# A decode kernel's weight loads: 16 rows of one load per layer moved to three transfer engines, and W2's last 64 rows loaded over 16

## The chip, the cores and the metric

The kernel runs on one core of one Trainium2 chip. The metric is device time in microseconds (us) of one execution; lower is better. The five engines of a core are called PE (matrix products; PEld is its weight load), DVE (vector), ACT (scalar, which also issues loads), POOL and SP (which only issues loads here). Loads from the chip's main memory are carried out by 16 transfer engines that all issuers share.

## The reference

One token goes twice through an attention block with a cache of 8192 positions and an MLP. All is float32.

```python
def _A_ref(x, k_cache, v_cache, wq, wo):            # x [1, 1, 640]; caches [1, 32, 8192, 128]
    q = (x @ wq).reshape(B, Sq, H, Dh).transpose(0, 2, 1, 3)     # 32 heads of 128
    scores = jnp.einsum("bhqd,bhkd->bhqk", q, k_cache) * (Dh ** -0.5)
    p = softmax(scores)
    o = jnp.einsum("bhqk,bhkd->bhqd", p, v_cache)
    return o.transpose(0, 2, 1, 3).reshape(B, Sq, H * Dh) @ wo   # wo [4096, 640]

def _B_ref(x, w1, w2):                              # w1 [640, 1728], w2 [1728, 640]
    return jnp.maximum(x @ w1, 0) @ w2

x = A_x
for layer in range(2):                              # both layers: the same caches and weights
    x = x + _A_ref(layernorm(x), k_cache, v_cache, wq, wo)
    x = x + _B_ref(layernorm(x), w1, w2)
```

K and V of one layer have 268 MB, so the caches alone, read once per layer, are most of the 573.76 MB that the kernel moves.

## The kernel before

**The stream of K and V.** SP issues nearly nothing but loads of K and V into `ring`, one large buffer of 128 partitions (`pump`, L264). A load has 128 rows of 4 to 64 KB. The order of these loads is a list written ahead (`todo`); SP issues the next one as soon as its place in the ring is free, which PE sets by reading the pieces that lay there (`release`). Layer 0 goes through the heads 0 to 31, layer 1 through 31 to 0, so that the pieces of the last heads are kept from one layer to the next.

**A head.** For each head PE forms the scores (`scores`, L540), DVE and ACT the softmax (`exponentials`: L551, L556, L563, L565, L569, L571), PE the sum over V (`values`, L595; `late_values`, L613, for the last one), and DVE and PE its output column (L628 to L646).

**The weights of attention.** Heads stand in eight groups of four. `pair` is one buffer of 128 partitions with two halves, each for the weights of one group: `wqo` holds Wq and Wo of the eight groups side by side, so laid out that one load of two neighbouring groups brings Wo of one group and Wq of the next. Such a load (`load_pair`, L323, issued by ACT) has 128 rows of 2 x 10240 = 20480 bytes. When a group's first head is through, `run_out` multiplies the outputs of the group before with Wo (`projected`, L510) and then issues the next load into `pair`; two heads later `queries_by_halves` (L467, L476, L481) reads Wq of the group after. In layer 0 the first group of a load counts 0, 1, 2 and so on, in layer 1 it counts down.

**W1 and W2.** They are loaded once, in layer 0, by ACT, as the function `due` tells by the head's place: W1 (L838), most of the W2 rows that stay (L840, 128 rows), and W2's last 64 rows (L843). W2's other rows come in each layer through the ring as the last of SP's loads, and the last blocks of the MLP read them (`times_rows`, L498). The last 64 rows are stored in DRAM as two blocks of 8 x 5 rows, of which 8 x 4 are read; so each of the two loads has 32 rows of 2560 bytes, in eight runs of four.

**What sets the order.** Each engine works its instructions off in the order in which the program wrote them. A load gives a signal when all its bytes have landed. There are eight such signals (`DMAHW0` to `DMAHW7` in the listings below); all loads of SP and ACT use them in turn, and a load waits for the one that had its signal eight loads before.

Of the kernel before, what the change touches and what calls it, by code (L numbers as in the profile page):

```python
# [15 lines left out]
P = 128  # L16
D = 640
# [7 lines left out]
NG = H // HG  # L25
# [65 lines left out]
]  # L91
KEPT = 4024
W2_PLACES = 800
WIDE = 64
MIX_BEHIND = 3
MIX_AT = [10, 14, 18, 22]
# [19 lines left out]
def size(unit):  # L116
    return sum(wide(kind_of(unit, t), piece) for t, piece in enumerate(unit[1]))
# [4 lines left out]
F_TILES = 3  # L122
# [5 lines left out]
W2_ALL = [("w2", i) for i in range(len(W2_RUNS))]  # L128
RING = KEPT + W2_PLACES


@with_exitstack
def decode_kernel(ctx: ExitStack, tc: tile.TileContext, x, kv, wqo, w1, w2, w2_rest, w2_last, out):
    nc = tc.nc
    consts = ctx.enter_context(tc.tile_pool(name="consts", bufs=1))
    work = ctx.enter_context(tc.tile_pool(name="work", bufs=1))
# [60 lines left out]
    for row in ROWS:  # L197
        n = 8 * sum(size(UNITS[h][i]) for h, i in row)
        block = kv[o : o + P * n].rearrange("(p m) -> p m", p=P)
        o += P * n  # L200
        a = 0
# [4 lines left out]
    for u in W2_ALL:  # L206
        n = 8 * P * size(UNITS[u[0]][u[1]])
# [91 lines left out]
    pair = consts.tile([P, 2, NB * HG * DH], F32, name="pair")  # L299

    def chain(g, i):

        return (g + i) % 2

    def as_wq(half):
        return pair[:, half].rearrange("p (c n) -> p c n", c=NB)

    def as_wo(half):
        return pair[:, half].rearrange("p (j n) -> p j n", j=HG)

    def load_wq(g, queue):
        wq_t[g] = as_wq(1)
        queue.dma_start(pair[:, 1], wqo[chain(g, 0)][:, g])

    def load_pair(g_o, g_q):

        if g_q is None:
            n = D if g_o == 0 else 0
            nc.scalar.dma_start(pair[:, 0, n:], wqo[chain(g_o, 1)][:, g_o, n:])
            wo_t[g_o] = as_wo(0)  # L320
            return
        first = min(g_o, g_q)
        nc.scalar.dma_start(  # L323
            pair.rearrange("p a n -> p (a n)"),
            wqo[chain(g_o, 1)][:, first : first + 2].rearrange("p a n -> p (a n)"),
        )
        wo_t[g_o] = as_wo(g_o - first)
        wq_t[g_q] = as_wq(g_q - first)

# [25 lines left out]
    w2_t = consts.tile([P, F_REST, D], F32, name="w2_t")  # L355
# [300 lines left out]
    def sums_of_rows(pt, rows, last, some=range(4)):  # L656
        for r in some:
            nc.tensor.matmul(
                pt[:, :WIDE],
                rows[:, r],  # L660
                ind[:, r : r + 1].to_broadcast([P, WIDE]),
                start=(r == 0),
# [77 lines left out]
    def attention_and_mlp(L, xr, s):  # L740
# [3 lines left out]
        groups = [run[0] // HG for run in runs]  # L744
# [14 lines left out]
        if L:  # L759
            load_wq(groups[1], nc.scalar)  # L760
        else:
            load_pair(groups[0], groups[1])

        chores, slow = [], []

# [12 lines left out]
        def run_out(k):  # L778

            projected(times_halves, acc, runs[k], o_cols[k], k == 0, k == NG - 2)  # L780
            yield "dve"
            load_pair(groups[k + 1], groups[k + 2] if k + 2 < NG else None)
            if k < NG - 2:
                return
            rows = work.tile([P, RUN], F32, name="p")[:64, : 2 * DR]
            nc.vector.tensor_copy(rows, acc[:64, : 2 * DR])
            pt = ps_m.tile([P, 512], F32, name="px")
            for g in range(4):
                nc.tensor.matmul(
                    pt[32 * g : 32 * g + 32, :DR],  # L790
                    sel[:64, g // 2 : g // 2 + 1].to_broadcast([64, 32]),
                    rows[:, g % 2 * DR : (g % 2 + 1) * DR],
                    start=True,
                    stop=True,
                )
            yield "dve"
            nc.vector.scalar_tensor_tensor(xr, pt[:, :DR], 1.0, xr, op0=ALU.mult, op1=ALU.add)
# [26 lines left out]
        def due(h):  # L824

            where = heads.index(h)
            k, j = divmod(where, HG)
            if j == 0:
                o_cols[k] = work.tile([P, HG], F32, name="o_cols", bufs=2)
                sums[k] = work.tile([P, 4 * HG], F32, name="sums", bufs=2)  # L830
            if where and j == 0:
                chores.append([run_out(k - 1), "pe"])
            if j == 2 and k + 1 < NG:
                slow.append([queries_of(k + 1), "pe"])
            if where == H - 2:
                chores.append([first_of_last(), "pe"])
            if L == 0 and where == 4:
                nc.scalar.dma_start(w1_t, w1)  # L838
            if L == 0 and where == 7:
                nc.scalar.dma_start(w2_t[:, 0], w2_rest)  # L840
            if L == 0 and where in (12, 13):
                a = 32 * (where - 12)
                nc.scalar.dma_start(w2_t[a : a + 32, 1], w2_last[where - 12, :, :4])  # L843
            if where == 7:
                of, nth = divmod(last, HG)
                if L:
                    make_identity(nc, ident)
                    n = D // 8
                    assert is_free(RING - n, n)
                    live["last"] = RING - n, n  # L850
                raw = ring[:, 8 * RING - D :] if L else mix[:, :D]
                nc.scalar.dma_start(raw, wqo[chain(of, 1)][:, of, nth * D : (nth + 1) * D])
                wo_last.append(raw if L else as_wo(0)[:, nth])
            if where == 8:
                slow.append([mixing(wo_last[-1] if L else mix[:, :D]), "dve"])
            if where in MIX_AT:
                slow.append([mixing_quarter(MIX_AT.index(where)), "pe"])
# [21 lines left out]
        for where, h in enumerate(heads[:-1]):  # L879
# [24 lines left out]
            k, j = divmod(where, HG)  # L904
# [14 lines left out]
            if near_end:  # L919
                rows = copied_rows(hd)  # L920
# [43 lines left out]
        rows = copied_rows(hd)  # L964
        at_once(rest)
        pt = ps_m.tile([P, 512], F32, name="pm")
        for a, (piece, at) in enumerate(pieces[2:]):
# [6 lines left out]
        nc.tensor.matmul(  # L974
            pt[:, :WIDE], o_late, one_of_each.to_broadcast([P, WIDE]), start=False, stop=True
        )
# [18 lines left out]
        for j in range(F_TILES):  # L995
            pj = bank_tile() if j else ps_m.tile([P, 512], F32, name="pt")
            nc.tensor.matmul(
                pj[:, :WIDE].rearrange("p (a g) -> p a g", g=4),
                hr[:, j * P : (j + 1) * P],
                sel[:, None, :4].to_broadcast([P, WIDE // 4, 4]),  # L1000
                start=True,
# [42 lines left out]
        for a, b in enumerate(blocks):  # L1044
# [13 lines left out]
            rows = 2 * half if b == nb + 1 else P  # L1058
            if b < nb:
                i = next(i for i, run in enumerate(W2_RUNS) if b in run)  # L1060
                where = L, ("w2", i), b - W2_RUNS[i][0]
                tile_of, at = at_of[where]
# [45 lines left out]
def _laid_out(A_x, A_k_cache, A_v_cache, A_wq, A_wo, B_w1, B_w2):  # L1108
    k = np.asarray(A_k_cache)[0].reshape(H, 4, 4, RUN, DH).transpose(0, 4, 1, 2, 3)
    v = np.asarray(A_v_cache)[0].reshape(H, 4, 4, NBL, 4, 32, DH)  # L1110
    v = v.transpose(0, 1, 5, 4, 2, 3, 6).reshape(H, P, 4, 4, NBL, DH)
    kv = np.empty(H * P * SK * 2, k.dtype)
    o = 0
    for row in ROWS:
        n = 8 * sum(size(UNITS[h][i]) for h, i in row)
        block = kv[o : o + P * n].reshape(P, n)
        o += P * n
        a = 0
        for h, i in row:
            unit = UNITS[h][i]  # L1120
            for t, piece in enumerate(unit[1]):
                if kind_of(unit, t) == "k":
                    r, c, m = piece
                    part = k[h, :, :, r, c : c + m]
                else:
                    b, r, m = piece
                    part = v[h, :, :, r : r + m, b]
                part = part.reshape(P, -1)
                block[:, a : a + part.shape[1]] = part
                a += part.shape[1]  # L1130
    rows = np.zeros((P, FB, D), np.asarray(B_w2).dtype)
    for b, f in enumerate(_hidden_rows()):
        rows[f >= 0, b] = np.asarray(B_w2)[f[f >= 0]][:, _COLS]
    w2 = np.concatenate([rows[:, run[0] : run[-1] + 1].reshape(-1) for run in W2_RUNS])
    wq = np.asarray(A_wq).reshape(NB, P, NG, HG * DH).transpose(2, 1, 0, 3).reshape(NG, P, -1)
    wo = np.asarray(A_wo)[:, _COLS].reshape(NG, HG, DH, D).transpose(0, 2, 1, 3).reshape(NG, P, -1)
    wqo = np.empty((2, P, NG, wq.shape[2]), wq.dtype)
    for g in range(NG):
        wqo[g % 2, :, g] = wq[g]
        wqo[1 - g % 2, :, g] = wo[g]  # L1140
    w2_last = np.zeros((2, 8, 5, D), rows.dtype)
    w2_last[:, :, :4] = rows[:64, 4 * F_TILES + 1].reshape(2, 8, 4, D)
    return {
        "x": np.repeat(np.asarray(A_x).reshape(D)[_COLS].reshape(4, DR), 32, axis=0),
        "kv": kv,
        "wqo": wqo,
        "w1": np.asarray(B_w1).reshape(NB, P, DFF).transpose(1, 0, 2),
        "w2": w2,
        "w2_rest": rows[:, 4 * F_TILES],
        "w2_last": w2_last,  # L1150
    }


# [22 lines left out]
```

## Time and profile before

| | |
|---|---|
| median of 3 runs | 1345.72 us (1345.54 to 1348.48) |
| the profiled execution | 1345.14 us, of which the span from the first to the last instruction is 1343.4 |
| busy, share of the span | PE 63%, PEld 20%, DVE 18%, ACT 4%, POOL 0% |
| moved | 573.76 MB, mean 427 GB/s |
| chain that ended last | DMA 62%, PE 28%, DVE 6% |

A page's DMA share is the mean busy share of the 16 transfer engines: 1.00 means that all work, 0.50 that eight do. It can read a little over 1 in a short stretch. `q1` is the queue of SP's loads, `q10` that of ACT's, `q8` and `q14` bring the program's own instructions. Each of the 16 engines has its own share of each queue, and one that has work from two queues takes from them in turn. In the chain, a line is a step that released the next one. The PE column of the clock says what share of its full speed PE was granted.

### The profile page before, as it was taken

How to read it: one execution, taken by the hardware profiler on the slowest of the kernel's cores; microseconds unless marked ns; L12 is line 12 of the kernel's file. 1: busy time of each engine (PE TensorE's matmuls, PEld its weight loads, DVE VectorE, ACT ScalarE, POOL GpSimd, SP SyncE). 2: the span in 40 equal slices, each digit the busy share in tenths (PEclk: the TensorE clock that was granted, in tenths of full speed). 3: DMA queues.
4: the chain of work that ended last, by engine and by line, in shares of the span. 5: the costliest groups of instructions: out<-in, count | busy, mean ns of one | idle time of the engine just before them, and what ended most of it. 6: DMA issues, size and time to landing. Idle time of an engine off the chain costs nothing.

```text
span 1343.4 us, 13327 instructions
## 1 busy us (share of the span) xinstructions
PE 851.2 (63%) x5958; PEld 265.3 (20%) x5958; DVE 246.9 (18%) x774; ACT 59.1 (4%) x149; POOL 3.4 (0%) x12
## 2 busy tenths in 40 slices
PE   3464455655865665667787754556677566765678
PEld 1121111111211111112252211111122121211224
DVE  1121111111111121121222211221111111111222
ACT  0000000000000000000000000000000000000000
POOL 0000000000000000000000000000000000000000
PEclk8677777778787777777899877787878777777799
DMA  9999999999999999999999999999999999999997
GB/s 414 430 427 443 421 443 421 441 421 431 435 432 432 431 443 413 447 420 428 425 399 426 432 439 429 428 444 420 445 431 428 422 432 433 436 424 444 419 426 329
DMA packets 20737, 573.76 MB, mean 427 GB/s; under 512 B 2308, under 2 KB 2440, under 8 KB 4680
## 3 DMA queue, kind: packets, MB, share of 16 engines
q1 hardware_dynamic: 17576, 529.57, 91.7%
q10 hardware_dynamic: 3104, 43.34, 7.6%
q8 instruction: 47, 0.77, 0.2%
q14 instruction: 10, 0.08, 0.0%
HBM read 572.90 MB, written 0.00 MB: 426 GB/s over the span
## 4 chain that ended last, share of the span: by engine, by line
DMA 62%; PE 28%; DVE 6%; ACT 1%; issue 1%; another core or an unknown queue 1%; ACTq 0%; SPq 0%; DVEq 0%
DMA ring<-in_kv 61%; PE ps L540 13%; PE outs L595 10%; DVE pt L569 2%; DVE sums L551 2%; ACT p L565 1%; PE pm L556 1%; DVE p L632 1%; DVE pT L571 1%; DMA mix<-in_w 0%; DVE sums L563 0%; PE acc L510 0%; PE px L498 0%; PE px L467 0%
## 5 line engine op out<-in xcount | busy, mean ns | idle before, releaser
L540 PE MATMUL ps<-ring,spread_q 128*32 128x512 f32 (+4 forms) x2088 | 315.2, 752 | 235.1 <-DMA ring<-in_kv 231.9
L595 PE MATMUL outs<-ring,pT 128*4 128x512 f32 (+1 forms) x2032 | 324.0, 794 | 137.7 <-DVE pT L571 102.3
L540 PEld LDWEIGHTS ps<-ring,spread_q 128*32 128x32 f32 x2088 | 76.8, 135 | 419.8 <-issue 309.3
L551 DVE TENSOR_REDUCE sums<-ps 128x1 f32<-128x512 f32 x64 | 44.2, 691 | 537.5 <-PE ps L540 537.5
L595 PEld LDWEIGHTS outs<-ring,pT 128*4 128x4 f32 x2032 | 57.2, 103 | 343.3 <-issue 231.1
L565 ACT ACTIVATE p<-ps,sums 128x512 f32<-128x512 f32 x64 | 44.0, 687 | 1137.1 <-DVE sums L563 1137.1
L628 DVE TENSOR_SCALAR p<-outs,small 128x128 f32<-128x128 f32 x60 | 21.0, 351 | 333.6 <-PE outs L595 333.6
L632 DVE SCALAR_TENSOR_TENSOR p<-outs,small,p 128x128 f32<-128x128 f32 x180 | 63.1, 351 | 6.4
L556 PE MATMUL pm<-row_of,sums 128*128 128x16 f32 x128 | 26.1, 280 | 49.6 <-DVE sums L551 48.8
L569 DVE STREAM_TRANSPOSE pt<-p 128x512 f32<-128x512 f32 x64 | 46.5, 726 | 57.8 <-ACT p L565 57.8
L642 PE MATMUL pm<-small,p 128*128 128x1 f32 x120 | 22.3, 255 | 38.1 <-DVE p L632 24.9
L556 PEld LDWEIGHTS pm<-row_of,sums 128*128 128x128 f32 x128 | 19.8, 194 | 108.5 <-DVE sums L551 106.8
L716 PE MATMUL px<-w_t,wct 128*128 128x448 f32 (+1 forms) x80 | 39.0, 572 | 0.0
L510 PE MATMUL acc<-pair,o_cols 128*32 128x320 f32 x224 | 33.9, 447 | 0.0
L642 PEld LDWEIGHTS pm<-small,p 128*128 128x128 f32 x120 | 18.7, 190 | 72.0 <-DVE p L632 42.7
L467 PE MATMUL px<-pair,ln_xc 128*32 128x256 f32 x280 | 32.6, 379 | 0.0
L467 PEld LDWEIGHTS px<-pair,ln_xc 128*32 128x32 f32 x280 | 16.1, 110 | 21.1 <-issue 9.8
L510 PEld LDWEIGHTS acc<-pair,o_cols 128*32 128x32 f32 x224 | 13.4, 114 | 25.2 <-issue 24.4
L646 DVE COPY o_cols<-pm 128x1 f32<-128x1 f32 x56 | 8.9, 158 | 46.8 <-PE pm L642 46.8
L563 DVE TENSOR_REDUCE sums<-pm 128x1 f32<-128x16 f32 x64 | 11.2, 175 | 32.9 <-PE pm L556 32.9
L571 DVE COPY pT<-pt 128x64 f32<-128x64 f32 x64 | 14.3, 223 | 2.2
L481 PE MATMUL px<-small,p 64*128 64x2 f32 x56 | 8.1, 246 | 9.9 <-DVE p L476 9.9
(136 smaller groups left out, 218.1 us busy)
## 6 DMA issues: line engine op xcount, KB each, us to landing
ring<-in_kv SPq DMA_DIRECT2D x28, 4096.0 KB, 30.6
ring<-in_kv SPq DMA_DIRECT2D x11, 6144.0 KB, 34.3
ring<-in_kv SPq DMA_DIRECT2D x27, 2048.0 KB, 32.4
pair<-in_wqo ACTq DMA_DIRECT2D x13, 2560.0 KB, 29.2
ring<-in_w SPq DMA_DIRECT2D x4, 1280.0 KB, 27.9
w_t<-in_w ACTq DMA_DIRECT2D x1, 4320.0 KB
ring<-in_kv SPq DMA_DIRECT2D x4, 1024.0 KB, 7.5
ring<-in_kv SPq DMA_DIRECT2D x1, 3200.0 KB, 20.1
```

The lines of the kernel that those rows point to most:

```text
L467: nc.tensor.matmul(pq[32 * j : 32 * j + 32, :n], xc[:, c : c + 1].to_broadcast([P, 32]), wq_t[g][:, c, j * n : (j + 1) * n], start=(c == 0 ...
L510: nc.tensor.matmul(acc[32 * half : 32 * half + 32, : 2 * DR], col.to_broadcast([P, 32]), wt[:, 2 * half * DR : 2 * (half + 1) * DR], start ...
L540: nc.tensor.matmul(hd.ps[32 * g : 32 * g + 32, c : c + n], spread_q[:, 3 - r : 35 - r], tile_of[:, at + g * n : at + (g + 1) * n], start=f ...
L551: nc.vector.tensor_reduce(hd.nm, hd.ps, AX.X, ALU.max, negate=True)
L556: nc.tensor.matmul(pt[:, :16], hd.nm.to_broadcast([P, P]), row_of.rearrange("p g r -> p (g r)"), start=True, stop=True,)
L565: nc.scalar.activation(hd.p, hd.ps, AF.Exp, bias=hd.low, scale=1.0, accum_out=hd.l)
L569: nc.vector.transpose(pt, hd.p)
L571: nc.vector.tensor_copy(hd.pT.rearrange("p (c r) -> p c r", r=4), pt.rearrange("p (c r) -> p c r", r=32)[:, :, :4],)
L595: nc.tensor.matmul(hd.out[32 * g : 32 * g + 4, r : r + m].rearrange("p r d -> p (r d)"), hd.pT[:, 4 * i : 4 * i + 4], tile_of[:, v : v + m ...
L632: nc.vector.scalar_tensor_tensor(oc[:, r], hd.out[:, r], ind[:, r : r + 1], oc[:, r - 1], op0=ALU.mult, op1=ALU.add,)
L642: nc.tensor.matmul(pt[:, :1], oc[:, 3], ones, start=True, stop=True)
L716: nc.tensor.matmul(pt[:, :n], wct[:, c], w1_t[:, c, f : f + n], start=(c == 0), stop=(c == NB - 1),)
```

## The change

In each layer, one of the loads of two groups is split. In layer 0 it is the load whose first group is 4, in layer 1 the one whose first group is 2 (`THREES`: place in the new array, half of `wqo`, first group). Of its 128 rows, 112 are loaded as before from `wqo`; 15 rows (112 to 126) from a new array `wqo_three`, which holds them as 3 x 6 rows of which 3 x 5 are read; and the last row alone, from `wqo`. W2's last 64 rows are stored plainly and loaded by one load of 64 rows, where the first of the two loads stood.

```diff
+THREES = {(0, 4): (0, 1, 4), (1, 2): (1, 0, 2)}
...
-    def load_pair(g_o, g_q):
+    def load_pair(L, g_o, g_q):
...
         first = min(g_o, g_q)
-        nc.scalar.dma_start(
-            pair.rearrange("p a n -> p (a n)"),
-            wqo[chain(g_o, 1)][:, first : first + 2].rearrange("p a n -> p (a n)"),
-        )
+        where = pair.rearrange("p a n -> p (a n)")
+        rows = wqo[chain(g_o, 1)][:, first : first + 2].rearrange("p a n -> p (a n)")
+        if (L, first) in THREES:
+            at, i, _ = THREES[L, first]
+            assert i == chain(g_o, 1)
+            nc.scalar.dma_start(where[: P - 16], rows[: P - 16])
+            nc.scalar.dma_start(where[P - 16 : P - 1], wqo_three[at, :, :5])
+            nc.scalar.dma_start(where[P - 1 :], rows[P - 1 :])
+        else:
+            nc.scalar.dma_start(where, rows)
...
-            if L == 0 and where in (12, 13):
-                a = 32 * (where - 12)
-                nc.scalar.dma_start(w2_t[a : a + 32, 1], w2_last[where - 12, :, :4])
+            if L == 0 and where == 12:
+                nc.scalar.dma_start(w2_t[:64, 1], w2_last)
...
-    w2_last = np.zeros((2, 8, 5, D), rows.dtype)
-    w2_last[:, :, :4] = rows[:64, 4 * F_TILES + 1].reshape(2, 8, 4, D)
+    wqo_three = np.zeros((2, 3, 6, 2 * wq.shape[2]), wq.dtype)
+    for at, i, g in THREES.values():
+        wqo_three[at, :, :5] = wqo[i, P - 16 : P - 1, g : g + 2].reshape(3, 5, -1)
...
-        "w2_last": w2_last,
+        "w2_last": rows[:64, 4 * F_TILES + 1],
+        "wqo_three": wqo_three,
```

On ACT in layer 0, from W2's last rows to the load of two groups that is split, the program stood so before (instruction, destination and source, shape of the destination, and the signals waited for):

```order
18 L843 DMA w_t<-in_w_last 32x1x640 [waits DMAHW2_49]
19 L565 ACTIVATE p,sums<-ps,sums 128x512 [waits DVE_49,Activation_49]
20 L323 DMA pair<-in_wqo 128x5120 [waits DMAHW5_49,PE_49]
21 L843 DMA w_t<-in_w_last 32x1x640 [waits DMAHW6_49]
22 L565 ACTIVATE p,sums<-ps,sums 128x512 [waits DVE_49,Activation_49]
23 L724 COPY mix<-px 128x448 [waits PE_49]
24 L565 ACTIVATE p,sums<-ps,sums 128x512 [waits DVE_49,Activation_49] x3
25 L323 DMA pair<-in_wqo 128x5120 [waits DMAHW5_49,DMAHW4_49,PE_49]
26 L565 ACTIVATE p,sums<-ps,sums 128x512 [waits DVE_49,Activation_49]
```

and stands so now:

```order
18 L849 DMA w_t<-in_w_last 64x640 [waits DMAHW2_49]
19 L572 ACTIVATE p,sums<-ps,sums 128x512 [waits DVE_49,Activation_49]
20 L333 DMA pair<-in_wqo 128x5120 [waits DMAHW5_49,PE_49]
21 L572 ACTIVATE p,sums<-ps,sums 128x512 [waits DVE_49,Activation_49]
22 L731 COPY mix<-px 128x448 [waits PE_49]
23 L572 ACTIVATE p,sums<-ps,sums 128x512 [waits DVE_49,Activation_49] x3
24 L329 DMA pair<-in_wqo 112x5120 [waits DMAHW5_49,DMAHW3_49,PE_49]
25 L330 DMA pair<-in_wqo_three 15x1x5120 [waits DMAHW4_49]
26 L331 DMA pair<-in_wqo 1x5120 [waits DMAHW6_49]
27 L572 ACTIVATE p,sums<-ps,sums 128x512 [waits DVE_49,Activation_49]
```

One of W2's two loads is gone, and the load of two groups has become three, ahead of the same exponential (L565, now L572). In layer 1 the same three stand in the place of one.

On PE, the first reader of that load is the query product of the next group (`px<-pair`, L467, now L474), behind a head's `values` and ahead of the next head's scores. Before:

```order
167 L595 MATMUL outs_102<-ring,pT 4x512 x15
168 L467 MATMUL px<-pair,ln_xc 32x256 [waits DMAHW4_49,Activation_49]
169 L467 MATMUL px<-pair,ln_xc 32x256 x9
170 L642 MATMUL pm<-small,p 128x1 [waits DVE_49]
171 L481 MATMUL px<-small,p 128x2 [waits DVE_49,PE_49]
172 L481 MATMUL px<-small,p 128x2
173 L540 MATMUL ps<-ring,spread_q 32x512 [waits DMAHW6_49]
```

and now:

```order
167 L602 MATMUL outs_102<-ring,pT 4x512 x15
168 L474 MATMUL px<-pair,ln_xc 32x256 [waits DMAHW4_49,DMAHW6_49,DMAHW3_49,Activation_49]
169 L474 MATMUL px<-pair,ln_xc 32x256 x9
170 L649 MATMUL pm<-small,p 128x1 [waits DVE_49]
171 L488 MATMUL px<-small,p 128x2 [waits DVE_49,PE_49]
172 L488 MATMUL px<-small,p 128x2
173 L547 MATMUL ps<-ring,spread_q 32x512 [waits DMAHW7_49]
```

It waits for three loads in the place of one; the order on PE is the same.

More of the change, by code (lines that the diff above doesn't have):

```diff
@@ L132, in decode_kernel @@
 @with_exitstack
-def decode_kernel(ctx: ExitStack, tc: tile.TileContext, x, kv, wqo, w1, w2, w2_rest, w2_last, out):
+def decode_kernel(ctx: ExitStack, tc: tile.TileContext, x, kv, wqo, w1, w2, w2_rest, w2_last, wqo_three, out):
     nc = tc.nc
@@ L761, in attention_and_mlp @@
         else:
-            load_pair(groups[0], groups[1])
+            load_pair(L, groups[0], groups[1])
         chores, slow = [], []
@@ L781, in run_out @@
             yield "dve"
-            load_pair(groups[k + 1], groups[k + 2] if k + 2 < NG else None)
+            load_pair(L, groups[k + 1], groups[k + 2] if k + 2 < NG else None)
             if k < NG - 2:
```

## The prediction

> **What bounds the kernel now.** I read the page first: its DMA part (busy tenths and mean rate, then the queues with packets, MB and share of the 16 transfer engines' span) and the issues with KB and median us to landing.
>
> ```profile
> span 1343.4 us, 13327 instructions
> ...
> DMA packets 20737, 573.76 MB, mean 427 GB/s; under 512 B 2308, under 2 KB 2440, under 8 KB 4680
> ...
> q1 hardware_dynamic: 17576, 529.57, 91.7%
> q10 hardware_dynamic: 3104, 43.34, 7.6%
> q8 instruction: 47, 0.77, 0.2%
> q14 instruction: 10, 0.08, 0.0%
> ...
> pair<-in_wqo ACTq DMA_DIRECT2D x13, 2560.0 KB, 29.2
> ```
>
> The shares add up to 99.5%: the 16 transfer engines work nearly all the time, q1 for SP's ring loads, q10 for ACT's weight loads. The bytes stay the same here, so only their distribution over the engines can matter. A load has landed when the last engine that takes part is done; the end is set by the latest engine, not by the mean.
>
> Next came the chain of work that ended last (start, us, step), and from the timeline the last wait of PE for a load.
>
> ```profile
> 1280.08 34.82 DMA ring<-in_kv
> ...
> 1324.30 0.74 DVE pt L569
> ...
> 1338.93 1.31 PE px L498 x32
> 1319.84 0.24 PEld L540 LDWEIGHTS ps<-ring,spread_q 128*32 128x32 f32 x8 [0.37 <-DMA ring<-in_kv]
> ```
>
> The reader is to see that the last K piece ends a DMA wait at 1319.84, and that 23.6 us of dependent work follow; the last blocks of W2 are read from 1338.93. Whatever moves the latest engine moves this tail one for one.
>
> How even the engines are is read from the DMA share at the end and at the layer boundary (columns: us, busy of PE, PEld, DVE, ACT, POOL, clock, DMA share, GB/s).
>
> ```profile
> 1332.00:1333.00 1.00, 0.69 (x17) 0.42 (x16) 0.22 (x1) 0.00 (x0) 0.00 (x0) 1.00 0.97 405
> 1333.00:1334.00 1.00, 0.90 (x14) 0.58 (x6) 0.60 (x3) 0.37 (x2) 0.00 (x0) 1.00 0.85 353
> 1334.00:1335.00 1.00, 1.00 (x23) 0.67 (x22) 0.37 (x3) 0.00 (x0) 0.00 (x0) 1.00 0.63 261
> 1335.00:1336.00 1.00, 1.00 (x34) 0.99 (x38) 0.21 (x2) 0.00 (x0) 0.00 (x0) 1.00 0.59 237
> 1336.00:1337.00 1.00, 1.00 (x32) 0.45 (x21) 0.33 (x2) 0.00 (x0) 0.00 (x0) 1.00 0.50 195
> 1337.00:1338.00 1.00, 1.00 (x26) 0.76 (x22) 0.34 (x2) 0.00 (x0) 0.00 (x0) 1.00 0.47 189
> 1338.00:1339.00 1.00, 0.99 (x22) 0.65 (x18) 0.49 (x4) 0.00 (x0) 0.00 (x0) 1.00 0.15 61
> ```
>
> ```profile
> 692.00:693.00 1.00, 0.93 (x16) 0.42 (x16) 0.24 (x3) 0.00 (x0) 0.00 (x0) 1.00 0.80 333
> 693.00:694.00 1.00, 0.90 (x12) 0.82 (x14) 0.58 (x4) 0.37 (x2) 0.00 (x0) 1.00 0.56 236
> ...
> 696.00:697.00 1.00, 1.00 (x23) 0.41 (x17) 0.30 (x2) 0.00 (x0) 0.00 (x0) 1.00 0.80 293
> ```
>
> Sixteen times one minus the share is the number of engines without work. At 1335 to 1336 that is 6.6: seven engines are through. Up to 1335 they have lost (0.03 + 0.15 + 0.37) x 16 = 8.8 engine-us, 1.3 each, so they end near 1333.7. About eight more stop between 1337 and 1339, the last by about 1338.9, just before the last W2 blocks are read. At the boundary of the layers again 0.44 x 16 = 7 engines have nothing to do, for (0.20 + 0.44 + 0.20) x 16 = 13.4 engine-us, 1.9 us each. An early engine thus has 1338.9 - 1333.7 + 1.9 = 7.1 us in hand over the whole program. No view says which engines these are.
>
> If all 16 ended together, the end would come earlier by the idle shares of the seven rows of the end added up, 2.84 us. That caps the gain.
>
> **The change part by part.** Price of a row: q10 moved 43.34 MB in 7.6% of 16 x 1343.4 us, or 1634 us, so 26.5 KB per us; a row of 20480 B takes 0.77 us, a W2 row of 2560 B 0.10. A ring row of 65536 B, from 529.57 MB in 91.7%, takes 2.44.
>
> How a load is split over engines: the page has 2308 packets under 512 B, which is 143 x 16 + 2 x 8 + 4, with 146 loads in the program. So one small packet per engine ends each load, W2's two loads of 8 x 4 rows ran on eight engines each, and the output of four rows on four. [...]
>
> I take the split by that count: 112 rows give each engine 7; 15 rows laid out as 3 x 5 give three engines 5 each; the one row left goes to one engine. Instead of 8 rows each, engine 0 gets 13, engines 1 and 2 get 12, and thirteen engines get 7. Over both layers, in us:
>
> - engine 0: +10 rows, +7.7; engines 1 and 2: +8 rows, +6.2; the others: -2 rows, -1.54.
> - W2's 64 rows: eight rows each on engines 0 to 7 become four rows on each of the 16: -0.39 for 0 to 7, +0.39 for 8 to 15.
> - Sum: engine 0 +7.3, engines 1 and 2 +5.8, engines 3 to 7 -1.9, engines 8 to 15 -1.15.
>
> Suppose that engines 0 to 2 are among the seven early ones. The late ones then end at 1338.9 - 1.15 = 1337.75. Engines 1 and 2 end at 1333.7 - 1.9 + 5.8 = 1337.6, level with them, and engine 0 at 1333.7 - 1.9 + 7.3 = 1339.1, if it loses all its idle time at the boundary. So the latest engine moves by something between -1.15 (engine 0 not last) and +0.2 (engine 0 last); I take the middle, -0.5 us.
>
> The load itself becomes later. It is issued as before, and its first reader and the work around it are these rows of the timeline (layer 0, then layer 1).
>
> ```profile
> 391.20 0.33 ACTq L323 DMA_DIRECT2D pair<-in_wqo  x1
> 399.87 0.69 ACT L565 ACTIVATE p<-ps,sums 128x512 f32<-128x512 f32 x1 [17.23 <-DVE sums L563]
> 420.17 6.49 PE L540 MATMUL ps<-ring,spread_q 128*32 128x512 f32 x32 [11.12 <-DMA ring<-in_kv]
> 434.81 2.32 PE L467 MATMUL px<-pair,ln_xc 128*32 128x256 f32 x20
> 439.53 5.34 PE L540 MATMUL ps<-ring,spread_q 128*32 128x512 f32 x32 [0.78 <-DMA ring<-in_kv]
> 1030.72 0.34 ACTq L323 DMA_DIRECT2D pair<-in_wqo  x1
> 1074.88 2.33 PE L467 MATMUL px<-pair,ln_xc 128*32 128x256 f32 x20
> DMA to landing us min/median/max: 7.5/30.7/50.7
> ```
>
> The last row is SP's ring loads. While both queues have work, a weight row follows a ring row on each engine, as 8 x (2.44 + 0.77) = 25.7 us against the 29.2 to landing bears out. Engine 0's five further rows therefore add at most 5 x 3.21 = 16.0 us: layer 0 lands at 391.20 + 29.2 + 16.0 = 436.4, 1.6 us after L467 wants it; layer 1 at 1075.9, 1.0 us after. PE waits there in order, and L642, L481 and the next head's L540 stand behind it. L540 already waited 0.78 us, so that head comes up to 1.6 us later and frees its ring slots later, and SP's next load with it. That costs nothing, because a ring load stands 30.7 us in the queue, while 8 MB at 427 GB/s take 19.6: some 11 us of work lie ahead of the engines. Without that cover it would be 2.6 us.
>
> ACT issues two loads more, 0.33 us each, before an exponential that came after 17.23 us of idle time; in layer 1 likewise. W2 takes one issue less. Zero. Each new load also waits for a load that stands eight places before it in the program, and later ring loads wait for these. Some 36 MB lie between the former, 84 us at 427 GB/s, and 24 MB or more between the latter, 56 us, both longer than any landing above. Zero.
>
> Sum: -0.5 us on the profiled execution's 1345.14, 1344.6. Its runs' median, 1345.72, is 0.58 above it: 1345.2. A measurement of this kernel can tell about 0.2%, 2.7 us, from no change.
>
> **The rivals.** *Slower: two engines write through one entrance.* In all loads of 128 rows an engine has eight rows of its own. With 112 rows cut by seven, and the rows from 112 to 126 on engines 0 to 2, an engine writes into rows that another engine serves otherwise. If both then share one entrance, the weight row takes 0.77 us longer and so does the ring row beside it, 1.54 per collision. The other engine is in a ring row for 2.44 of 3.21 us, 76% of the time: 0.76 x 7 x 1.54 = 8.2 us per load, 16 for both, 1361; at most 14 x 1.54 = 21.6, and nothing if the engines write independently. It decides from about 3.2 us, two collisions of fourteen. [...] Against it stands that nothing in this trace ever took such a form. Chance 0.22.
>
> *Slower: engines 0 to 2 are not all early.* Something delays the nine late engines, and q8's 47 packets of instructions, which go over the same engines, are a candidate; nothing ties them to engine numbers. If engine 0 is late, it ends 7.3 us later: 1353; with 1 or 2 alone, 5.8: 1351.5. [...] I give it 0.13.
>
> *No effect on distribution.* If the 15 rows or the single row are spread over more engines, the bytes are even again: between -1.5 and 0 us. It ends inside the forecast's bound; 0.10.
>
> *Faster by more than 2.7 us.* It would take nearly the whole 2.84 of the end, or a gain at the boundary that I don't see: 1342.5; 0.05.
>
> **How the numbers follow.** Forecast 0.50, no effect on distribution 0.10: within 0.2%, 0.60. Entrance 0.22 and late engines 0.13: slower, 0.35. Faster 0.05. The likeliest time is 1345.2, its own range 1343.6 (-1.15, and some tenths between runs) to 1347.0. The range for 8 in 10 goes from 1343.6 to 1357: it takes in the late engines and the lower half of the entrance's prices, and leaves out 0.05 below and some 0.13 above.
>
> **What would show it.** Right: by the DMA share, fewer than seven engines stop before 1336 and the fall is steeper; q1 and q10 keep 91.7% and 7.6%; small packets rise from 2308 to about 2316. Shared entrance: GB/s falls well under 427 in the slices at 395 to 440 and 1034 to 1075 while the share stays at 1, and weight rows cost over 0.77 us, so q10's share rises. Late engines: one to three engines, 0.06 to 0.19 of share, run on alone for over 5 us at the end. Wrong altogether would be a wait of PE for the weights near 434 that passes on to the ring.

## The result, and the profile after

The changed kernel takes 1383.73 us (median of 6 runs, 1380.87 to 1389.98) against 1345.72 before: 1.0286 times as long, 95% interval 1.0263 to 1.0309. That is 38 us slower, where the forecast was 1345.2 and the range ended at 1357. The profiled execution has a span of 1381.3 us.

The page first: span, rate in 40 slices of 34.5 us, packets, the two queues, the split loads' median us to landing, and the group of the query products (busy, mean ns, idle before it).

```profile
span 1381.3 us, 13334 instructions
...
GB/s 420 424 425 444 424 439 419 444 405 436 433 348 316 391 430 437 437 421 424 430 411 430 432 438 427 428 439 431 433 426 339 294 433 431 437 418 446 419 424 330
DMA packets 20744, 573.75 MB, mean 415 GB/s; under 512 B 2316, under 2 KB 2448, under 8 KB 4688
...
q1 hardware_dynamic: 17576, 529.57, 91.3%
q10 hardware_dynamic: 3112, 43.34, 8.0%
...
L474 PE MATMUL px<-pair,ln_xc 128*32 128x256 f32 x280 | 34.5, 395 | 10.2 <-DMA pair<-in_wqo 10.2
...
pair<-in_wqo ACTq DMA_DIRECT2D x2, 2240.0 KB, 42.2
```

The rate has two holes, 348, 316 and 391 in the slices from 380 us on and 339 and 294 from 1036 on: just where the two split loads run. Bytes and shares of the queues are nearly as before. The window rows say more (before, then after; the last two numbers are DMA share and GB/s).

```profile
400.00:430.00 30.00, 13.53 (x70) 3.47 (x70) 4.45 (x13) 1.95 (x5) 0.00 (x0) 0.71 1.02 441
1052.00:1082.00 30.00, 16.98 (x124) 5.51 (x124) 4.00 (x12) 0.78 (x2) 0.00 (x0) 0.77 1.03 443
```

```profile
400.00:430.00 30.00, 8.98 (x65) 2.52 (x56) 3.46 (x10) 1.31 (x3) 0.00 (x0) 0.73 0.98 273
1052.00:1082.00 30.00, 11.55 (x54) 2.63 (x54) 3.46 (x10) 1.31 (x3) 0.00 (x0) 0.65 1.02 261
```

The transfer engines are as busy as before, 0.98 and 1.02, but move 273 and 261 GB/s instead of 441 and 443. They are not idle and not uneven: each transfer takes longer. How long is read from the two queues at 400 to 425 us (packets, MB, share of 16 engines' 25 us), before and after.

```profile
q1 hardware_dynamic: 154, 9.04, 83.6%
q10 hardware_dynamic: 114, 2.01, 18.8%
```

```profile
q1 hardware_dynamic: 80, 5.24, 72.5%
q10 hardware_dynamic: 80, 1.64, 26.8%
```

A ring row of 65536 B took 0.836 x 400 / 9.04 = 37.0 us per MB, or 2.42 us, before, and 0.725 x 400 / 5.24 = 55.3, or 3.63 us, after. A weight row of 20480 B went from 0.77 to 1.34 us.

Where the time was lost is told by the same small step of each head, DVE's minimum over the maxima (L563, now L570), ahead of and behind each hole. Before, then after:

```profile
381.58 0.17 DVE L563 TENSOR_REDUCE sums<-pm 128x1 f32<-128x16 f32 x1 [0.49 <-PE pm L556]
531.02 0.17 DVE L563 TENSOR_REDUCE sums<-pm 128x1 f32<-128x16 f32 x1 [0.49 <-PE pm L556]
1022.79 0.18 DVE L563 TENSOR_REDUCE sums<-pm 128x1 f32<-128x16 f32 x1 [0.49 <-PE pm L556]
1151.91 0.17 DVE L563 TENSOR_REDUCE sums<-pm 128x1 f32<-128x16 f32 x1 [0.49 <-PE pm L556]
```

```profile
384.19 0.17 DVE L570 TENSOR_REDUCE sums<-pm 128x1 f32<-128x16 f32 x1 [0.49 <-PE pm L563]
550.96 0.17 DVE L570 TENSOR_REDUCE sums<-pm 128x1 f32<-128x16 f32 x1 [0.49 <-PE pm L563]
1039.60 0.17 DVE L570 TENSOR_REDUCE sums<-pm 128x1 f32<-128x16 f32 x1 [0.49 <-PE pm L563]
1190.39 0.17 DVE L570 TENSOR_REDUCE sums<-pm 128x1 f32<-128x16 f32 x1 [0.49 <-PE pm L563]
```

The lag is 2.6, 19.9, 16.8 and 38.5 us: some 17 and 22 us at the two split loads (single heads scatter by 3), and next to nothing elsewhere.

### The profile page after: what moved, and what is told of

The parts are those of the page before. It is cut to its first block, busy times and chain, and to the rows that moved or that the text cites. A ratio compares the mean times of both kernels' runs of the same rounds, so it can differ in the third digit from the quotient of the medians.

```text
span 1381.3 us, 13334 instructions
## 1 busy us (share of the span) xinstructions
PE 833.8 (60%) x5958; PEld 264.9 (19%) x5958; DVE 247.2 (18%) x774; ACT 59.2 (4%) x149; POOL 3.4 (0%) x12
## 2 busy tenths in 40 slices
DMA packets 20744, 573.75 MB, mean 415 GB/s; under 512 B 2316, under 2 KB 2448, under 8 KB 4688
## 4 chain that ended last, share of the span: by engine, by line
DMA 60%; PE 28%; DVE 6%; another core or an unknown queue 3%; ACT 1%; issue 1%; ACTq 0%; SPq 0%; DVEq 0%
DMA ring<-in_kv 59%; PE ps L547 13%; PE outs L602 10%; DVE sums L558 2%; DVE pt L576 2%; ACT p L572 1%; DMA pair<-in_wqo 1%; PE pm L563 1%; DVE p L639 1%; PE px L474 1%; DVE pT L578 1%; DMA mix<-in_w 0%; PE px L505 0%; DVE sums L570 0%
## 5 line engine op out<-in xcount | busy, mean ns | idle before, releaser
L602 PE MATMUL outs<-ring,pT 128*4 128x512 f32 (+1 forms) x2032 | 308.8, 761 | 133.5 <-DVE pT L578 99.5
L572 ACT ACTIVATE p<-ps,sums 128x512 f32<-128x512 f32 x64 | 44.0, 687 | 1178.6 <-DVE sums L570 1178.6
L563 PE MATMUL pm<-row_of,sums 128*128 128x16 f32 x128 | 26.1, 280 | 49.6 <-DVE sums L558 48.8
L474 PE MATMUL px<-pair,ln_xc 128*32 128x256 f32 x280 | 34.5, 395 | 10.2 <-DMA pair<-in_wqo 10.2
L563 PEld LDWEIGHTS pm<-row_of,sums 128*128 128x128 f32 x128 | 19.8, 194 | 108.5 <-DVE sums L558 106.8
L474 PEld LDWEIGHTS px<-pair,ln_xc 128*32 128x32 f32 x280 | 17.0, 115 | 32.5 <-issue 22.2
L570 DVE TENSOR_REDUCE sums<-pm 128x1 f32<-128x16 f32 x64 | 11.2, 175 | 32.8 <-PE pm L563 32.8
L723 PEld LDWEIGHTS px<-w_t,wct 128*128 128x128 f32 x80 | 12.0, 190 | 11.6 <-issue 11.6
```

The source lines that it names most:

```text
L474: nc.tensor.matmul(pq[32 * j : 32 * j + 32, :n], xc[:, c : c + 1].to_broadcast([P, 32]), wq_t[g][:, c, j * n : (j + 1) * n], start=(c == 0 ...
L563: nc.tensor.matmul(pt[:, :16], hd.nm.to_broadcast([P, P]), row_of.rearrange("p g r -> p (g r)"), start=True, stop=True,)
L572: nc.scalar.activation(hd.p, hd.ps, AF.Exp, bias=hd.low, scale=1.0, accum_out=hd.l)
L602: nc.tensor.matmul(hd.out[32 * g : 32 * g + 4, r : r + m].rearrange("p r d -> p (r d)"), hd.pT[:, 4 * i : 4 * i + 4], tile_of[:, v : v + m ...
L723: nc.tensor.matmul(pt[:, :n], wct[:, c], w1_t[:, c, f : f + n], start=(c == 0), stop=(c == NB - 1),)
```

## The experiments

Words used below. *Slow rows* are weight rows that took over 0.9 us, counted from the trace's records of single packets (start, duration, queue, size); undisturbed ones take 0.76 or 0.77. The records name no engine, so no run shows which engine writes which row. Where the prediction or an expectation numbers engines, maps rows to them or speaks of an engine's own rows, that is the author's assumption, and a row is *foreign* where by that assumption another engine writes it than in a load of 128 rows, as all ring loads are. For the first fourteen runs the assumption was rows 8e to 8e+7 for engine e.

| run | split loads as | median us | ratio to before (95%) | slow rows of 128, layer 0 / 1 |
|---|---|---|---|---|
| after | 112, 3 x 5, 1; W2 in one | 1383.73 | 1.0263 to 1.0309 | 126 / 126 |
| e1 | 112, 3 x 5, 1 | 1382.35 | 1.0255 to 1.0286 | 128 / 127 |
| e2 | rows 0-63, 64-127 | 1384.59 | 1.0272 to 1.0302 | 128 / 128 |
| e3 | even rows, odd rows | 1345.97 | 0.9987 to 1.0006 | 0 / 0 |
| e4 | 112, 16 | 1382.73 | 1.0252 to 1.0291 | 127 / 128 |
| e5 | whole; W2 in one | 1346.87 | 0.9999 to 1.0018 | 0 / 0 |
| e6 | 64, 32, 16, 15, 1 | 1360.87 | 1.0101 to 1.0131 | 32 / 30 |
| e7 | even rows; odd in halves | 1365.98 | 1.0134 to 1.0164 | 64 / 64 |
| e8 | the same, lower odd rows 8 x 4 | 1370.98 | 1.0167 to 1.0201 | 64 / 64 |
| e9 | 8, 8, 64, 32, 16 | 1360.70 | 1.0094 to 1.0128 | 46 / 46 |
| e10 | whole, a head later | 1348.85 | 1.0014 to 1.0051 | 0 / 1 |
| e11 | whole, 17 us later | 1345.78 | 0.9989 to 1.0008 | 1 / 0 |
| e12 | 64, 16 x4 / 32 x4 | 1356.79 | 1.0064 to 1.0098 | 63 / 0 |
| e13 | whole, in 16 runs of 8 | 1381.68 | 1.0248 to 1.0279 | 128 / 128 |
| e14 | whole, in 32 runs of 4 | 1345.68 | 0.9987 to 1.0006 | 0 / 0 |
| e15 | 8 x 4, 8 x 4, 64 | 1377.76 | 1.0226 to 1.0256 | 88 / 80 |

Two more, e16 and e17, are at the end. In all but the changed kernel and e5, W2's last rows are loaded as before.

**Where the loss comes from: e1 to e4.** e1 keeps the split loads and undoes the W2 edit. e2 to e4 replace the three loads:

```diff
-            nc.scalar.dma_start(where[: P - 16], rows[: P - 16])        # 112, then 15 and 1
+            nc.scalar.dma_start(where[:64], rows[:64])                  # e2, two halves
+            nc.scalar.dma_start(where[64:], rows[64:])
...
+            nc.scalar.dma_start(where[0::2], rows[0::2])                # e3, every second row
+            nc.scalar.dma_start(where[1::2], rows[1::2])
...
+            nc.scalar.dma_start(where[: P - 16], rows[: P - 16])        # e4, 112 rows and 16
+            nc.scalar.dma_start(where[P - 16 :], rows[P - 16 :])
```

> Only the weight loads are split (112 + 15 + 1 rows, both layers); W2's last 64 rows stay in two loads of 32 rows. Theory A (an engine that writes into rows which another engine serves in a load of 128 rows slows that engine's ring row and its own): nearly the whole loss is here, 1380 to 1384 us, since the heads up to the first split load drift by 3 us at most. Theory B (the ten or eight rows more on engines 0 to 2): the same number, this run can't part them. Theory D (the W2 load matters): under 1375.

> Both split loads as two loads of 64 rows, rows 0 to 63 and rows 64 to 127; every engine gets four rows of each, eight in all, as in one load of 128. Theory A: engine e writes rows 4e to 4e+3, which lie in the eight rows of another engine (all but the first and the last engine): 1360 to 1385, with the moved bytes per us falling under 350 GB/s near 400 and 1050 us. Theory B (uneven engines): bytes are even, 1345.7, within 2.7. Theory C (more loads, more signals waited for, a later landing): under 1350, and the same as with every second row.

> Both split loads as two loads of 64 rows again, but one takes rows 0, 2, 4 and so on, the other rows 1, 3, 5 and so on; engine e then gets four of the rows 8e to 8e+7 in each, rows that it serves in a load of 128. Theory A: no collision, 1345.7 within 2.7, and 427 GB/s near 400 and 1050 us. Theory B: the same. Theory C: as slow as with two halves. Theory S (it is the reading side, the cut of the rows in main memory): slow as well, over 1355, as the rows that an engine reads are cut differently here too.

> Both split loads as 112 rows and 16 rows, each over all 16 engines: seven rows and one row for each engine, even bytes, no engine with more. Theory A: the 112 rows cut by seven collide as in the changed kernel and the last 16 rows all lie in the rows of the last two engines: 1365 to 1382, the bigger part of the loss of 38 us. Theory B: 1345.7 within 2.7, as no engine has more rows than before.

e2 and e3 have the same number of loads, rows per load, bytes, issues and signals; they differ only in which rows each load takes. One loses 39 us, the other nothing. Windows of e2, then of e3:

```profile
410.00:430.00 20.00, 0.00 (x0) 0.00 (x0) 0.00 (x0) 0.00 (x0) 0.00 (x0) 0.56 1.02 269
1055.00:1075.00 20.00, 11.18 (x54) 2.59 (x54) 3.46 (x10) 1.31 (x3) 0.00 (x0) 0.60 0.97 246
```

```profile
410.00:430.00 20.00, 7.42 (x38) 2.02 (x42) 1.90 (x5) 0.78 (x2) 0.00 (x0) 0.63 1.01 433
1055.00:1075.00 20.00, 10.46 (x58) 2.62 (x62) 1.90 (x5) 0.78 (x2) 0.00 (x0) 0.61 0.99 423
```

The theory of uneven engines falls: e2 and e4 were meant to give every engine eight rows, the share in their first hole is 1.02 and 1.01, so no engine idles, and they lose as much. So does that of more loads and later landings: e3 has more loads as well, and in e2 and e4 PE never waited for the weights (idle before L473 0.0 on both pages). What is left is how the rows are cut into loads: by theory A which engine handles which row, by the place in the buffer that it writes to or by the rows of main memory that it reads. These runs can't part the two, because a cut sets both. e16 and e17 at the end part them for small loads: they read the same rows in the same form, and differ only in the place written to.

**Price and size: e5 to e8.** e5 is the W2 edit alone. The split loads of the others:

```diff
+            nc.scalar.dma_start(where[0::2], rows[0::2])                # e6
+            nc.scalar.dma_start(where[1::4], rows[1::4])
+            nc.scalar.dma_start(where[3::8], rows[3::8])
+            nc.scalar.dma_start(where[7 : P - 1 : 8], wqo_three[at, :, :5])
+            nc.scalar.dma_start(where[P - 1 :], rows[P - 1 :])
...
+            nc.scalar.dma_start(where[0::2], rows[0::2])                # e7; e8 has the second as
+            nc.scalar.dma_start(where[1:64:2], rows[1:64:2])            # wqo_eight[at, :, :4], 8 x 4 rows
+            nc.scalar.dma_start(where[65::2], rows[65::2])
```

> Only W2's last 64 rows change (one load of 64 rows over 16 engines instead of two loads of 8 x 4 rows); no weight load is split. Theory A: 64 rows of 2560 B cut by four collide, but a row is an eighth of a weight row's bytes: four rows that each cost an eighth of 2.3 us, 1.2 us, less what the two loads of before cost in the same way: 1345 to 1348. Rival (the price is one per row, whatever its bytes): 4 x 2.3 us more, 1353 to 1356.

> The same shift of rows to engines 0 to 2 as in the changed kernel (15 rows as 3 x 5, one row alone), but of each eight rows the first seven are read by the engine that serves them in a load of 128 (loads of 64, 32 and 16 rows with steps of 2, 4 and 8), and only row 8e+7 goes to engines 0 to 2. Theory A, price per foreign row: one foreign row per engine instead of eight, 18.5/8 = 2.3 us per load less 0.77 for the row that the engine no longer has; engines 0 to 2 with five rows more lose some 6 us per load if they are the last: 1348 to 1358. Rival (bytes per engine alone, as in the prediction): 1344 to 1347. Rival (any foreign row spoils a load): 1375 or more.

> Both split loads as 64 rows (every second, each to its own engine) and two loads of 32 rows (the odd rows of the lower and of the upper half, two rows per engine, all but four of them foreign). Four foreign rows for most engines instead of eight, bytes even. Theory A, price per foreign row: half of 37 us, 1361 to 1368. Rival (a load is spoilt as a whole, or by its length): 1375 or more. Rival (it takes a whole load's overlap): under 1352.

> As with half of the rows, but the odd rows of the lower half are stored as 8 x 5, of which 8 x 4 are read, so that engines 0 to 7 read them, each its own rows; the odd rows of the upper half are read by all 16 engines, two each, and are foreign. So four foreign rows lie in the rows of each of engines 8 to 15, none in those of 0 to 7, which read two rows more (1.5 us per load). If the latest engine sets the time: as with half of the rows, 1358 to 1366. If the mean over the engines does: a half of that, 1353 to 1357. If engines 0 to 7, which write the foreign rows too, pay as much as those whose rows they are: 1361 to 1368.

e7, with 64 slow rows per layer instead of 128, loses 20.0 us, half of e2's 38.6: between these two the loss goes with the number of slow rows. e5 can't be told from no change; the W2 edit's part is at most 2.4 us. e6 and e8 lose more than theory A (a foreign row slows itself and the ring row beside it) said, 14.9 and 25.0 us. The slow rows say why: in e6 there are 32 (30), not 16, which are just the load of 16 rows, the 15 and the one; in e8 the 32 rows of the 8 x 4 load, which the expectation called own rows, are slow as well. The assumption of rows 8e to 8e+7 doesn't account for these counts.

**Which loads are clean: e9, e12 to e15.**

```diff
+    (slice(0, 64, 8), slice(64, 128, 8)),                          # e9: EIGHTS[0]
+    (slice(0, 128, 16), slice(8, 128, 16)),                        # e9: EIGHTS[1]
...
+            for part in EIGHTS[L]:
+                nc.scalar.dma_start(where[part], rows[part])
+            for part in (slice(1, P, 2), slice(2, P, 4), slice(4, P, 8)):
+                nc.scalar.dma_start(where[part], rows[part])
...
+            # e12, layer 0: rows 0::2, 1::8, 3::8, 5::8, 7::8; layer 1: rows 0::4, 2::4, 1::4, 3::4
...
+            nc.scalar.dma_start(where, wqo_runs[at, :, :8])             # e13, stored as 16 x 9 rows
...
+            nc.scalar.dma_start(where, wqo_runs[at, :, :4])             # e14, stored as 32 x 5 rows
...
+            for i in range(2):                                          # e15, stored as 8 x 5 rows
+                nc.scalar.dma_start(where[32 * i : 32 * i + 32], wqo_runs[at, i, :, :4])
+            nc.scalar.dma_start(where[64:], rows[64:])
```

> On which engines does a load of fewer than 16 rows run? Of each split load 112 rows go to their own engines (loads of 64, 32 and 16 rows with steps); ahead of them stand two loads of eight rows, one row per engine: rows 0, 8, to 56 and rows 64, 72, to 120 in layer 0; rows 0, 16, to 112 and rows 8, 24, to 120 in layer 1. A row of weights takes 0.77 us where no other engine writes into the same eight rows, over 0.9 where one does. If eight rows run on engines 0 to 7: rows 0 to 56 are no foreign rows, the other three loads are (but for a row or two). If they run on every second engine: one of the two loads of layer 1 is clean, both of layer 0 collide. If on engines 8 to 15: rows 64 to 120 are clean. If on changing engines: none is clean. The time: one foreign row for some or all engines per load, 2.3 us each and up to one row more for eight engines: 1347 to 1354.

> Each row is meant for the engine that serves it in a load of 128. Layer 0: 64 rows (every second, four per engine) and four loads of 16 rows (rows 1, 9, 17 and so on, then 3, 11, and so on: one row per engine, each in another engine's eight rows). Layer 1: four loads of 32 rows (every fourth, two per engine). Theory A with the rows dealt out in order whatever their number: no row of weights over 0.9 us, 1346 within 2.7. Rival (a load with only one row per engine is dealt out otherwise, as the slow last 16 rows with eight rows to an engine's own hint): layer 0 has 64 slow rows and loses 8 to 10 us, layer 1 has none and loses nothing, 1354 to 1357. Rival (many loads in a row lose time in themselves): both layers lose alike.

> Each split load is one load of 128 rows again, but its source is stored as 16 x 9 rows of which 16 x 8 are read: 16 runs of eight rows, one run per engine, the rows of each run those that the engine serves in a plain load of 128. If rows are dealt out in order: no slow row of weights, 1345.7 within 2.7. If a load with one run per engine is dealt out otherwise (as the loads of 16 rows, of eight rows and of 8 x 4 rows suggest): 128 slow rows in each layer, and as slow as the changed kernel, 1378 to 1388.

> The same with the source stored as 32 x 5 rows of which 32 x 4 are read: 32 runs of four rows, two runs per engine. If rows are dealt out in order, or if only loads with one run per engine are dealt out otherwise (loads of 32 rows, two per engine, were clean): no slow row, 1345.7 within 2.7. If any source in runs spoils the order: as slow as e13.

> Each split load as rows 0 to 31 in eight runs of four, rows 32 to 63 in eight runs of four, and rows 64 to 127 plainly (64 rows, four per engine). Map 1 (engine e owns rows 8e to 8e+7): run j of four rows lies in the rows of engine j/2 or 4+j/2, so nearly all 128 rows are foreign and slow. [...] The time by map 1 as the changed kernel, 1378 to 1388; by map 2 eight foreign rows for engines 8 to 15 and four rows more for engines 0 to 7, 1365 to 1385, so the count of slow rows decides.

In e9 none of the four loads of eight rows was clean, and 14.8 us, more than expected, went with 16 rows per layer in such loads and 16 in a load of 16. e12 separates cleanly: the four loads of 16 rows are slow, the four loads of 32 rows in the other layer are not. Many loads in a row cost nothing; loads of 16 rows, every eighth, do. e13 and e14 are one load of all 128 rows each, the same rows in the same order to the same places. Stored as 16 runs, all 256 rows are slow; as 32 runs, none. Their median us to landing, e13 and then e14:

```profile
pair<-in_wqo_runs ACTq DMA_DIRECT2D x2, 2560.0 KB, 49.1
```

```profile
pair<-in_wqo_runs ACTq DMA_DIRECT2D x2, 2560.0 KB, 29.9
```

So in these runs a plain load of all 128 rows has at most one slow row (e5, e10, e11), and the cuts into even and odd rows (e3), into every fourth row (e12, layer 1) and the 32 runs (e14) have none; in the halves (e2), in 112 and 16 rows (e4), in the 16 runs (e13) and in the loads of 16 rows (e12) all rows are slow, but for one each in e4 and e12. Why the line runs there no run shows, as on no cut is it known which engine took which row.

e15 lies between: 88 and 80 of its 128 rows were slow. Even if all 64 rows of the plain load were, that leaves 24 (16) slow rows in the two 8 x 4 loads, and 40 (48) clean ones. Windows of three stretches in layer 0 show a slow one, a clean one and a slow one (DMA share, GB/s at the end):

```profile
396.00:414.00 18.00, 9.29 (x62) 2.37 (x54) 3.46 (x10) 1.31 (x3) 0.00 (x0) 0.84 1.02 284
...
420.00:428.00 8.00, 1.20 (x8) 0.46 (x12) 0.00 (x0) 0.00 (x0) 0.00 (x0) 0.50 0.96 416
431.00:450.00 19.00, 9.03 (x50) 1.77 (x42) 3.30 (x9) 0.78 (x2) 0.00 (x0) 0.68 1.06 281
```

The 40 and 48 clean rows speak against rows 8e to 8e+7, by which nearly all 128 were expected to be slow. The two forecasts of time, 1378 to 1388 and 1365 to 1385, overlap, and 1377.76 lies in the second; neither map is shown by a run. So these runs show that the cut of the rows (e2 against e3) and the form of their source (e13 against e14) matter; that two writers wait for one another at a shared entrance is a reading, not one that is shown.

**A late landing: e10 and e11.** The load is whole, but issued behind a later instruction of ACT:

```diff
-            nc.scalar.dma_start(where, rows)
+            late.append([2, lambda: nc.scalar.dma_start(where, rows)])  # e10: issued after the second exponential
+            late.append([1, lambda: nc.scalar.dma_start(where, rows)])  # e11: issued after the copy of the mix
```

> No load is split; the load of two groups that the change splits is issued whole but one exponential later, 37 us after its old place, in both layers, so that it lands near 458 and 1098 us, and PE waits some 23 us for it in front of the next head's scores. Theory C (a late landing passes on to the ring): if the 11 us of queued ring loads cover the first part of a wait, 12 us per layer remain, 1368 to 1372; without that cover 1385 to 1392; if a late landing is no loss, because the engines bring the weights at another time instead, under 1350.

> As before, but the load is issued some 17 us later, behind the copy of the mix on ACT, and lands near 438 and 1079 us: PE waits 3 to 4 us for it. The prediction's cover of 11 us: no loss, 1344 to 1348. Without cover: 3 to 4 us per layer, 1352 to 1354.

The query products behind the late loads, of e10 in both layers and then of e11 in layer 0:

```profile
442.13 4.24 PE L473 MATMUL px<-pair,ln_xc 128*32 128x256 f32 x20 [12.39 <-DMA pair<-in_wqo]
1088.08 3.83 PE L473 MATMUL px<-pair,ln_xc 128*32 128x256 f32 x20 [19.21 <-DMA pair<-in_wqo]
```

```profile
440.58 4.18 PE L473 MATMUL px<-pair,ln_xc 128*32 128x256 f32 x20 [11.06 <-DMA pair<-in_wqo]
```

31.6 us of waits cost 3.0 us (1.9 to 6.9) in e10. In e11 layer 0 waited 11.1 us, not the 3 to 4 expected, and layer 1 not at all; that cost nothing that can be measured. So the 10.2 us for which PE waits in the changed kernel are not its loss.

**Are engines 0 to 2 early: e16 and e17.** No load is split; six loads of no use are added in layer 0, into `mix` before it is first used:

```diff
+            if L == 0 and where in (1, 3, 5):
+                nc.scalar.dma_start(mix[:12], more[:, :4])              # e16; e17: mix[64:76]
+                nc.scalar.dma_start(mix[32:44], more[:, :4])            # e16; e17: mix[96:108]
```

> No load is split. Engines 0 to 2 get work of no use besides: six loads of 12 rows of 6912 B, as three runs of four (rows 0 to 11, and rows 32 to 43), into a buffer that is free in the first six heads of layer 0, overwritten before it is read; 24 rows, 6.2 us for each of the three engines. [...] If engines 0 to 2 are early and have 7 us in hand (the prediction): 1344 to 1348. If one of them is late: 1350 to 1353. If the three hold up the ring at that place whatever they have in hand at the end: 1350 to 1353 too, with the drift appearing before 150 us.

> [...] Theory A: three engines of the upper half lose what the six loads collide: 24 rows of 6912 B, a third of a weight row each, at a third of 1.8 to 2.3 us, 14 to 18 us over three heads, less what the ring's queue covers: 4 to 16 us slower than with the own rows. Rival (the place of the rows doesn't matter for so small loads): as with the own rows, within 2.7 us.

e16: 1348.28 us, 1.0011 to 1.0030 times before. e17: 1355.90, 1.0062 to 1.0092. The bytes, the source and the issues are the same; the place alone costs 7.6 us, inside the expected 4 to 16 over what the expectation calls the own rows, e16's rows 0 to 11 and 32 to 43. In e16 all 72 rows took 0.26 us, and of the ring rows of 65536 B between 20 and 220 us 15 of 729 took over 2.6 us (before: 4 of 747); in e17 it is 176 of 696. Which engines the loads ran on no run shows; that they were three is an estimate from the changed kernel's load of 3 x 5 rows, which ended in three small packets. The price of 72 rows of 0.26 us, by that estimate 6.2 us more for each of three engines, is 2.7 us in e16, some 40% of it, between the cases of the expectation. Where it arose is read from the same step as above, at the head behind the sixth load and at the last head, before and then e16:

```profile
166.29 0.17 DVE L563 TENSOR_REDUCE sums<-pm 128x1 f32<-128x16 f32 x1 [0.49 <-PE pm L556]
1323.22 0.17 DVE L563 TENSOR_REDUCE sums<-pm 128x1 f32<-128x16 f32 x1 [0.49 <-PE pm L556]
```

```profile
171.61 0.18 DVE L563 TENSOR_REDUCE sums<-pm 128x1 f32<-128x16 f32 x1 [0.49 <-PE pm L556]
1330.15 0.17 DVE L563 TENSOR_REDUCE sums<-pm 128x1 f32<-128x16 f32 x1 [0.49 <-PE pm L556]
```

The lag is 5.3 us behind the loads and 6.9 at the end: most of it is there at once. The profiled execution was the slowest of e16's ten, so the place can be read from it, but not the price.

No kernel here beats the one before.

## Why the prediction was wrong, step by step

- **The step that failed** is the sum over bytes: "a row of 20480 B takes 0.77 us", whichever engine writes it wherever. In the changed kernel's split load it took 1.34, and the ring row beside it 3.63 instead of 2.42. The right signs stood in the text with the first rival, with a chance of 0.22, because "nothing in this trace ever took such a form". That a form has not been seen is no evidence that it is harmless. The one odd form that the trace does hold, W2's loads of 8 x 4 rows, ran undisturbed (0.10 us for a row, 0.11 at most), while the 32 rows of e8's 8 x 4 load were slow: one such form told nothing of another. That two engines share an entrance, the rival's mechanism, no run shows.
- **The rival's own price was half of the truth**: 8.2 us per load, 16 for both and at most 21.6, against 38. It had 0.77 us more for the weight row and 0.77 for one ring row, for 76% of seven foreign rows. In fact nearly every weight row was slow (126 of 128), and the ring rows stayed slow all the while. Before, the records have 124 ring rows of 65536 B beside the 128 weight rows of layer 0's load (394.6 to 419.6 us), nearly one for one. The hole of e4, as one window:

```profile
396.00:443.00 47.00, 14.12 (x100) 3.98 (x92) 4.82 (x13) 2.09 (x5) 0.00 (x0) 0.71 1.01 262
```

  In 47 us at 262 GB/s one of the 16 engines moves 770 KB on average, eight weight rows and 9.2 ring rows. By the records of single packets e4's weight rows took 1.41 us there, 0.64 more than undisturbed, and its ring rows of 65536 B 3.91, 1.49 more: 8 x 0.64 + 9.2 x 1.49 = 18.8 us, the whole 18 to 19 per load. So 13.7 of it is lost in ring rows, for which the rival had 4.1, half of its 8.2.
- **The split by count was right**: 2316 small packets, as forecast, of which the split load of layer 0 has 20: 16, 3 and 1 for its three loads. W2's 64 rows ended in 16, its 8 x 4 rows before in 8 each. The numbers of the engines are another matter: that the 13 and 12 rows fell to engines 0 to 2 and W2's eight each to engines 0 to 7, from which the sum's +7.3, +5.8, -1.9 and -1.15 come, no run shows; in their place the runs showed 1.34 us for a weight row (400 to 425 us) and the loss of 38 us.
- **Early engines with 7.1 us in hand**: that engines 0 to 2 are such, and can take more rows anywhere in the program, is not borne out. In e16 an estimated 6.2 us more for each of three cost 2.7, and the lag arose where the loads ran. In layer 0 PE's wait for the split load ended at 459.63, behind the load's last small packet at 459.02; by estimate the latest engine sets when a load is through, so time that an engine has in hand at the end need not help before; whether the three have it is not shown. A shift of rows by the prediction's arithmetic would not have been free, even without collisions. At the end of the changed kernel the DMA share falls later and more steeply, as forecast for the shifted rows; the idle shares of the last six rows sum to 2.10, against 2.81 before, some 0.7 us if one execution each can tell it:

```profile
1372.00:1373.00 1.00, 1.00 (x34) 0.73 (x30) 0.21 (x2) 0.00 (x0) 0.00 (x0) 1.00 0.74 307
1373.00:1374.00 1.00, 1.00 (x35) 0.69 (x24) 0.33 (x3) 0.00 (x0) 0.00 (x0) 1.00 0.67 277
```

- **The late landing** was mis-sized (first reader at 459.63 after a wait of 9.2 us, instead of 436.4 and 1.6), but its cover was right, and better than said: e11's wait of 11 us cost nothing. The 11 us were reckoned for a ring load of 8 MB. The 28 loads of 4096 KB on the page before took 30.6 us to land and need 9.8 of their own at 427 GB/s, so by estimate some 21 us of work lay ahead of them.
- **Issues and signals at zero** were right: e3 cost nothing, and through the four loads of e12's layer 1 the lag stayed where it was (12.7 us at the head before them, 11.8 at the last head).
- **W2's edit at 0.39 us or less**: e5 gives 0.9, with no change inside its interval. 13 of its 64 rows took over 0.12 us, none before.
- **What would show it** did: the rate fell to 261 and 273 GB/s in the places named while the share stayed at 1, and q10's share rose from 7.6% to 8.0%.

## What to carry to other kernels

Before a load that runs beside a full-rate stream is cut, run the cut by itself and count its slow rows; in these runs a cut by every second or every fourth row had none (e3; e12, layer 1), and loads of every eighth row or of blocks were slow (e12, layer 0, 63 rows; e2, 128 in each layer). The DMA share alone hides such a loss, since slowed transfers read as busy (1.02 at 261 GB/s here): hold it against the GB/s of the same window. And where a rival's price is open, the bound should come from what it does to the stream as well as to the load.

## What the runs showed of the hardware that I had not expected

- How a source is stored can cost as much as how a load is split: the same 128 rows took 29.9 us to land as 32 runs of four and 49.1 us as 16 runs of eight, and with the latter the kernel took 36 us longer. All 256 rows were slow in the one form, none in the other.
- Loads whose rows are nearly all slow (e2, e4: 256 and 255 of 256) cost 18 to 19 us each of a stream at 430 GB/s, though 128 rows at 0.77 us are but 6.2 us of work for each of 16 engines.
- This stream takes a wait of its consumer lightly: 31.6 us of PE's waits cost 3.0 in e10.
